# Separate raw tiles for two kinds of expert weights, and one partial result written out by a DMA of its own

## The chip, the cores and the metric

The kernel runs on one core of a Trainium2 chip. The metric is the device time of one execution in microseconds (us). The engines are named as in the profile: PE is TensorE (PEld its weight load), DVE is VectorE, ACT is ScalarE, POOL is GpSimd, SP is SyncE, which here only issues DMAs. Each engine runs its own instructions in order and waits for the others by semaphores.

## What is computed

```python
def reference(**kwargs):
    ...
    attn_out = _attn_ref(**attn_kwargs)            # linear attention, 2 x 8 heads, 576 tokens, 64 wide
    x = np.ascontiguousarray(attn_out.transpose(0, 2, 1, 3)).reshape(B * S, H * D)   # 1152 x 512
    x = _moe_ref(x=x, **moe_kwargs)                # ((x @ w1) * (x @ w2)) @ w3 @ w_out
    return _moe2_ref(x=x, **moe2_kwargs)

def _moe2_ref(x, domain_probs, w1, w2):            # w1: 4 x 512 x 1024, w2: 4 x 1024 x 512
    p = domain_probs / (domain_probs.sum(-1, keepdims=True) + 1e-09)
    out = np.zeros((N, D), dtype=np.float32)
    for e in range(E):
        h = np.maximum(x @ w1[e], 0.0)
        out += p[:, e:e + 1] * (h @ w2[e])
    return out.astype(np.float32)
```

## The kernel before

The program has three stages that overlap at their borders. First the attention runs over eight pairs of heads, and beside it the weights of the gated block are loaded and prepared. Then `gated` forms the gated hidden activations, and `expert_input` multiplies them by the folded product of w3 and w_out; it is called twice, as c0 for batch 0 and c1 for batch 1, and its results are the tiles `x2`. Then come eight expert rounds: four experts, two halves of the hidden width each. Counted from 0, round 0 is `fresh` (it writes the result, the later ones add to it) and round 7 is `last`.

Every matrix is a float32r pair of a high part (made on ACT, line 79) and a low part (made on DVE, line 80, or on POOL); this is `split`, and a product takes three passes (`PASSES`). The matrix products of the expert rounds use a seven-product scheme in place of eight: `hidden` makes the products X1 to X7 and Y1 to Y7 in the order of the list `ORDER`, with sums and differences of blocks formed beforehand in place (line 586, in `raw` for the weights and in `hd` for the activations).

A round does this. `load_w1` loads two raw tiles (512 KB each, by SP, line 611), splits the first (`w1e`), splits a quarter (`w1f`), forms four sums in place, splits the second raw tile, forms more, and splits the first raw tile again: three `w1e` tiles of 8 KB per partition and one `w1f` tile of 4 KB. `hidden(w1t, 0)` and `hidden(w1t, 1)` multiply (line 690) and leave the activations in `hd`. `sums` splits them into `hs` and `hq`. `load_w2` loads two raw tiles and makes four `w2e` tiles. `second` multiplies by them (line 772), once for each half q of the main tokens, and `tails` does the remaining tokens (line 799).

All raw tiles come from one pool, `raw_p`, with three buffers, on the left side of the memory. The other tiles of the expert rounds lie on the right side, where the pools of the gated block (`w1_p`, eight tiles of 4 KB, then `w3_p`, eight tiles of 4 KB, then the temporaries `xq_p` of `expert_input`) are given back; a new tile waits for the old tiles under it (`reuse_waits="tile"`). The `w1e` pool of before takes 4 x 8 + 4 = 36 KB per partition there. The order of the instructions on each engine is set by a scheduler at build time.

In `second` a bank of the accumulator holds 512 columns. The bank of product 1 collects products 1, 6, 7 and 4 in its first half (a chain: each product is added to what the ones before left), and after each of these four steps the intermediate sum is read out, scaled by the routing weight. The row tile `o` (512 columns) of the one batch, `o1`, takes steps 1 and 6 (ACT, line 746) and then the whole bank of product 5 (DVE, line 749). The row tile of the other batch, `o5`, takes the result of product 5 (ACT) and, in its columns `D1`, step 7 of the chain on top (DVE, `add_scaled`, line 749); step 4 goes to its columns `D0` (ACT). A finished row tile is added to the output by a DMA that POOL issues (line 724, `add_to`), which waits for the DMA that wrote the same rows before. There are six `o` buffers, and nine row tiles in a round: four of `second` with q = 0, one of `tails`, four of `second` with q = 1. In round 7 the row tiles are read back from the output first, DVE adds all steps, and SP stores them.

Of the kernel before, what the change touches and what calls it, by code (L numbers as in the profile page):

```python
# [8 lines left out]
F32 = mybir.dt.float32  # L9
# [8 lines left out]
HS_BUFS = 4  # L18
O_BUFS = 6
# [25 lines left out]
def attention_moe_kernel(ctx: ExitStack, tc: tile.TileContext, q, k, v, omega, mw1, mw2, mw3, mwo, probs, ew1, ew2, out):  # L45
# [6 lines left out]
    P = 128  # L52
# [21 lines left out]
    def bank(tag):  # L74
        return ps_p.tile([P, 512], F32, tag=tag, name="ps_" + tag, bufs=BANKS[tag])
# [44 lines left out]
    def out_rows(t):  # L120

        if t == R:
            return [(slice(b * TAIL, (b + 1) * TAIL), slice(b * S + MAIN, (b + 1) * S, 1)) for b in range(B)]
        b, r = (0, t) if t < R else (1, t - R - 1)
        return [(slice(0, P), slice(b * S + r, b * S + MAIN, R))]
# [9 lines left out]
    w12, hid, wo, w3o, x2, xf = {}, {}, [], [], {}, {}  # L135
# [108 lines left out]
    with ExitStack() as actx:  # L244
        at = actx.enter_context(tc.tile_pool(name="at", bufs=2))
        st = actx.enter_context(tc.tile_pool(name="st", bufs=1))
        D1 = D + 1
# [73 lines left out]
        ps = bank("x")  # L321
        transpose(ps[:, :M], om_raw.rearrange("m j d -> m (j d)"))
        for j in range(2):
            s = slice(j * D, (j + 1) * D)
# [27 lines left out]
        class Pair:  # L352
# [81 lines left out]
            def place(self):  # L434
                ps = bank("et")
                for r in range(R):
                    transpose(ps[:, r * P:(r + 1) * P], self.xs[:, r].rearrange("p j d -> p (j d)"))
                x, s = xt[self.b][self.i], MAIN_COLS
                split(x[:, HI, s], x[:, LO, s], ps)
# [100 lines left out]
                    else:  # L540
                        gated(at, 2, int(s[1]), int(s[2]), ("w", "po") * 2)

    raw_p = ctx.enter_context(tc.tile_pool(name="raw", bufs=3, reuse_waits="tile"))
    h_p = mctx.enter_context(tc.tile_pool(name="h", bufs=2 * KF + 2 * KD - XT_BUFS, reuse_waits="tile"))
    a_p = cctx.enter_context(tc.tile_pool(name="a", bufs=1, reuse_waits="tile", side="right"))
    for s in AFTER.split():
# [23 lines left out]
    GH = KE // 4  # L570
    HD = DM // 2
    CH = 2 * P

    def right(name, bufs):
        return ctx.enter_context(tc.tile_pool(name=name, bufs=bufs, side="right", reuse_waits="tile"))

    w1e_p, w2_p, hid_p, hs_p, s_p, o_p = right("w1e", 4), right("w2e", 4), right("hid", 1), right("hs", HS_BUFS), right("s", 2), right("o", O_BUFS)
    hd = hid_p.tile([P, 2 * GH, B, S], F32, name="hd")
    turn = [0]

    def next_bank():
        turn[0] += 1
        return bank(("t", "f", "kv", "et", "f", "x", "w", "po")[turn[0] % 8])
# [4 lines left out]
    def parts(t, src):  # L588
        split(t[:, HI], t[:, LO], src)
        return t  # L590

    def combine(low, high, x11, x12, x21, x22, first, both):


        t = {}
        a = both(low)
        t["A11"], t["A12"] = a[0], a[1]
        t["A22"] = first(x22)
        place(x22, x21, x22, ALU.add)
        place(x21, x11, x21, ALU.subtract)  # L600
        a = both(high)
        t["S3"], t["S1"] = a[0], a[1]
        place(x11, x22, x11, ALU.subtract)
        place(x12, x12, x11, ALU.subtract)
        a = both(low)
        t["S2"], t["S4"] = a[0], a[1]
        return t

    def raw_half(src):
        r = raw_p.tile([P, 2, 512], F32, tag="raw", name="raw")  # L610
        nc.sync.dma_start(out=r.rearrange("p a (k f) -> p (a k) f", f=src.shape[2]), in_=src)
        return r

    def load_w1(hf):

        r = []
        for m in range(2):
            f0 = m * (EFF // 2) + hf * GH * P
            r.append(raw_half(ew1[e, :, f0:f0 + GH * P].rearrange("(k p) f -> p k f", p=P)))

        def both(src):
            t = parts(w1e_p.tile([P, 2, 2, 512], F32R, tag="w1e", name="w1e"), src)
            return [t[:, :, k].rearrange("p a (k f) -> p a k f", k=2) for k in range(2)]

        def first(src):
            t = parts(w1e_p.tile([P, 2, 512], F32R, tag="w1f", name="w1f", bufs=1), src)
            return t.rearrange("p a (k f) -> p a k f", k=2)

        return combine(r[0], r[1], r[0][:, 0], r[0][:, 1], r[1][:, 0], r[1][:, 1], first, both)

    def load_w2(hf):

        r = []
        for m in range(2):
            f0 = m * (EFF // 2) + hf * GH * P
            r.append(raw_half(ew2[e, f0:f0 + GH * P].rearrange("(g p) d -> p g d", p=P)))
        b = {(m, n): r[m][:, :, n * HD:(n + 1) * HD] for m in range(2) for n in range(2)}

        def both(src):
            return parts(w2_p.tile([P, 2, GH, DM], F32R, tag="w2e", name="w2e"), src)  # L640

        t = {}

        def named(x, one, two):
            t[one], t[two] = x[:, :, :, :HD], x[:, :, :, HD:]

        t["both"] = both(r[0]), both(r[1])
        named(t["both"][0], "B11", "B12")
        named(t["both"][1], "B21", "B22")
        place(b[0, 0], b[0, 1], b[0, 0], ALU.subtract)  # L650
        place(b[0, 1], b[1, 1], b[0, 1], ALU.subtract)
        named(both(r[0]), "T1", "T3")
        place(b[1, 1], b[1, 1], b[0, 0], ALU.subtract)
        place(b[1, 0], b[1, 0], b[1, 1], ALU.subtract)
        named(both(r[1]), "T4", "T2")
        return t
# [65 lines left out]
    def add_to(t, d, src, fresh):  # L722
        for n, (rows, toks) in enumerate(out_rows(t)):
            dma = nc.gpsimd.dma_start(out=out[toks, d], in_=src[rows], **({} if fresh else dict(accum_op=ALU.add))).ins  # L724
            if not fresh:
                tc.add_manual_dep(dma, added[t, n].name, after, reason="sum")
            added[t, n] = dma

    def results(t, last):

        o = o_p.tile([P, DM], F32, tag="o", name="o")
        if last:
            for n, (rows, toks) in enumerate(out_rows(t)):
                dma = nc.sync.dma_start(out=o[rows], in_=out[toks]).ins
                tc.add_manual_dep(dma, added[t, n].name, after, reason="sum")
        return o

    def store(t, src):
        for rows, toks in out_rows(t):
            nc.sync.dma_start(out=out[toks], in_=src[rows])  # L740

    def scaled(o, ps, t, last):
        if last:
            add_scaled(o, ps, t)
        else:
            nc.scalar.activation(out=o, in_=ps, func=ACTF.Copy, scale=pr[:, t, e:e + 1])  # L746

    def add_scaled(o, ps, t):
        nc.vector.scalar_tensor_tensor(out=o, in0=ps, scalar=pr[:, t, e:e + 1], in1=o, op0=ALU.mult, op1=ALU.add)  # L749

    D0, D1, DD = slice(0, HD), slice(HD, DM), slice(0, DM)

    def second(w2t, t, q, fresh, last):

        state = {}, {}
        finish = (lambda t, o: store(t, o)) if last else (lambda t, o: add_to(t, DD, o, fresh))
        if last:
            for j in range(2):
                for k, n in (("1", 0), ("5", R + 1)):
                    state[j]["o" + k] = results(n + q * 2 + j, True)  # L760
        for o in ORDER:
            j, k = "XY".index(o[0]), o[1]
            ta, tb = q * 2 + j, R + 1 + q * 2 + j
            now = state[j]
            if k in "15":
                now[k] = next_bank()
            bk = now["1" if k in "1674" else "5"]
            ps = bk[:, D1 if k in "53" else D0]
            a, b = NAMES[k]
            for g in range(GH):  # L770
                for n, (x, y) in enumerate(PASSES):
                    nc.tensor.matmul(  # L772
                        out=ps, lhsT=t[a][:, x, g, j * P:(j + 1) * P], rhs=w2t[b][:, y, g],
                        start=(k in "15" and g == 0 and n == 0), stop=(k in "234" and g == GH - 1 and n == 2),
                        skip_group_check=True,
                    )
            if k in "15" and not last:
                now["o" + k] = results(ta if k == "1" else tb, False)
            if k in "16":
                scaled(now["o1"][:, D0 if k == "1" else D1], ps, ta, last)  # L780
            elif k in "54":
                scaled(now["o5"][:, D1 if k == "5" else D0], ps, tb, last)
                if k == "4":
                    finish(tb, now["o5"])
            elif k == "3":
                add_scaled(now["o1"], bk, ta)
                finish(ta, now["o1"])
            elif k == "7":
                add_scaled(now["o5"][:, D1], ps, tb)

    def tails(w2t, fresh, last):

# [17 lines left out]
    for e in range(NE):  # L810
        for hf in range(2):
            fresh, last = e == 0 and hf == 0, e == NE - 1 and hf == 1
# [42 lines left out]
```

## Time and profile before

| | us |
|---|---|
| three runs | 694.33, 694.74, 696.3 |
| median | 694.74 |
| the profiled execution | 693.17 |
| its span, first to last instruction | 691.4 |
| PE busy | 665.8 |
| DVE busy | 482.7 |
| ACT busy | 402.9 |
| POOL busy | 163.8 |

The profiled execution lies 1.57 us under the median, and 1.8 us of it lie around the span. Busy times are sums over stages with different limits, so a stage is read by itself: which engine is without a gap there, and what the gaps of the others wait for. Times in the text are counted from the start of the span.

### The profile page before, as it was taken

How to read it: one execution, taken by the hardware profiler on the slowest of the kernel's cores; microseconds unless marked ns; L12 is line 12 of the kernel's file. 1: busy time of each engine (PE TensorE's matmuls, PEld its weight loads, DVE VectorE, ACT ScalarE, POOL GpSimd, SP SyncE). 2: the span in 40 equal slices, each digit the busy share in tenths (PEclk: the TensorE clock that was granted, in tenths of full speed). 3: DMA queues.
4: the chain of work that ended last, by engine and by line, in shares of the span. 5: the costliest groups of instructions: out<-in, count | busy, mean ns of one | idle time of the engine just before them, and what ended most of it. 6: DMA issues, size and time to landing. Idle time of an engine off the chain costs nothing.

```text
span 691.4 us, 12448 instructions
## 1 busy us (share of the span) xinstructions
PE 665.8 (96%) x4889; PEld 634.7 (92%) x4889; DVE 482.7 (70%) x782; ACT 402.9 (58%) x867; POOL 163.8 (24%) x155
## 2 busy tenths in 40 slices
PE   7898999999999999998999999999999999999997
PEld 6786778899999999998989999999999999999996
DVE  4888646669593222258987869877888688688795
ACT  5895445565452222246866676677676676686640
POOL 2865223259271000000021122230320311202200
PEclk9999999999999999999999999999999999999999
DMA  9764323235330000001143166372660762745715
GB/s 260 262 210 140 94 91 116 77 113 153 123 92 1 1 1 1 1 1 61 62 137 122 17 122 122 44 150 68 122 137 2 138 123 27 140 93 100 146 32 167
DMA packets 47146, 66.91 MB, mean 97 GB/s; under 512 B 7600, under 2 KB 30128, under 8 KB 47088
## 3 DMA queue, kind: packets, MB, share of 16 engines
q1 hardware_dynamic: 37792, 49.05, 22.8%
q0 software_dynamic: 8608, 16.52, 15.9%
q8 instruction: 38, 0.62, 0.4%
q10 hardware_dynamic: 688, 0.56, 0.3%
q14 instruction: 20, 0.16, 0.1%
HBM read 47.24 MB, written 18.87 MB: 96 GB/s over the span
## 4 chain that ended last, share of the span: by engine, by line
PE 73%; DVE 11%; DMA 6%; ACT 5%; issue 3%; POOL 1%; DVEq 0%; ACTq 0%; POOLq 0%; SPq 0%
PE ps_po L185 5%; PE ps_f L690 5%; PE ps_f L772 4%; DMA raw<-in_moe_w_dram 3%; PE ps_w L158 3%; PE ps_w L690 3%; PE ps_f L158 3%; PE ps_po L158 3%; PE ps_x L690 3%; PE ps_et L690 3%; PE ps_kv L690 2%; PE ps_t L690 2%; PE ps_po L690 2%; PE ps_kv L772 2%; PE ps_kv L412 2%
## 5 line engine op out<-in xcount | busy, mean ns | idle before, releaser
L724 POOL DMA_DIRECT2D out_dram<-o x70 | 57.7, 892 | 382.5 <-DVE o L749 206.6
L93 POOL TENSOR_SCALAR f64e<-f 128x512 f32<-128x512 f32 x40 | 66.8, 1673 | 78.1 <-DVE w3f L95 32.2
L80 DVE TENSOR_TENSOR hs<-hd,hs 128x1024 fp32r<-128x1024 f32 x48 | 58.4, 1219 | 3.1 <-ACT hs L79 2.4
L79 ACT ACTIVATE hs<-hd 128x1024 fp32r<-128x1024 f32 x48 | 50.7, 1056 | 7.9 <-DVE hd L586 4.9
L185 PE MATMUL ps_po<-wo,w3T 128*128 128x512 f32 x192 | 48.4, 400 | 3.3 <-DVE w3T L80 2.8
L690 PE MATMUL ps_f<-x,w1e 128*128 128x288 f32 x288 | 48.2, 298 | 3.1 <-DVE w1e L80 3.1
L674 ACT ACTIVATE hd<-hd 128x288 f32<-128x288 f32 x96 | 41.3, 439 | 15.6 <-DVE hd L672 14.9
L586 DVE TENSOR_TENSOR raw<-raw 128x512 f32<-128x512 f32 x64 | 43.9, 686 | 8.4 <-DMA raw<-in_moe_w_dram 8.1
L185 PEld LDWEIGHTS ps_po<-wo,w3T 128*128 128x128 f32 x192 | 34.8, 188 | 12.2 <-DVE w3T L80 3.9
L690 PEld LDWEIGHTS ps_f<-x,w1e 128*128 128x128 f32 x288 | 41.8, 191 | 3.7 <-DVE w1e L80 3.6
L94 DVE SCALAR_TENSOR_TENSOR f64e<-f,f64e 128x512 uint32<-128x512 uint32 x40 | 40.1, 1012 | 6.1 <-POOL f64e L93 5.8
L586 DVE TENSOR_TENSOR hd<-hd 128x512 f32<-128x512 f32 x64 | 43.9, 685 | 0.6
L79 ACT ACTIVATE w2e<-raw 128x1024 fp32r<-128x1024 f32 x32 | 33.5, 1058 | 17.7 <-PE ps_f L772 4.7
L772 PE MATMUL ps_f<-w2e,hs 128*128 128x256 f32 x288 | 42.6, 283 | 1.0 <-ACT o L746 0.6
L80 DVE TENSOR_TENSOR w2e<-raw,w2e 128x1024 fp32r<-128x1024 f32 x32 | 38.9, 1219 | 4.6 <-ACT w2e L79 4.5
L80 DVE TENSOR_TENSOR w1e<-raw,w1e 128x1024 fp32r<-128x1024 f32 x24 | 29.3, 1222 | 17.5 <-ACT w1e L79 17.2
L772 PEld LDWEIGHTS ps_f<-w2e,hs 128*128 128x128 f32 x288 | 38.1, 191 | 1.5 <-ACT o L746 0.8
L158 PE MATMUL ps_w<-xt,w 128*128 128x288 f32 x144 | 34.4, 298 | 0.0
L79 ACT ACTIVATE w1e<-raw 128x1024 fp32r<-128x1024 f32 x24 | 25.4, 1059 | 15.2 <-DMA raw<-in_moe_w_dram 10.3
L158 PE MATMUL ps_po<-xt,w 128*128 128x288 f32 x144 | 33.9, 296 | 0.0
L79 ACT ACTIVATE hid<-a 128x288 fp32r<-128x288 f32 x32 | 13.0, 440 | 30.8 <-DVE a L169 30.8
L80 POOL TENSOR_TENSOR w<-w12f,w 128x512 fp32r<-128x512 f32 x16 | 22.0, 1384 | 15.1 <-ACT w L79 15.0
(263 smaller groups left out, 1777.4 us busy)
## 6 DMA issues: line engine op xcount, KB each, us to landing
f<-in_moe_w_dram SPq DMA_DIRECT2D x32, 512.0 KB, 3.7
raw<-in_moe_w_dram SPq DMA_DIRECT2D x32, 512.0 KB, 5.5
out_dram<-o POOLq DMA_DIRECT2D x56, 256.0 KB, 5.2
f<-in_moe_w_out_dram SPq DMA_DIRECT2D x8, 512.0 KB, 5.1
kr<-in_k_dram SPq DMA_DIRECT2D x8, 256.0 KB, 3.8
vr<-in_v_dram SPq DMA_DIRECT2D x8, 256.0 KB, 5.0
o<-out_dram SPq DMA_DIRECT2D x8, 256.0 KB, 3.6
out_dram<-o SPq DMA_DIRECT2D x8, 256.0 KB, 2.5
```

The lines of the kernel that those rows point to most:

```text
L79: nc.scalar.activation(out=hi, in_=src, func=ACTF.Copy)
L80: (eng or nc.vector).tensor_tensor(out=lo, in0=src, in1=hi.bitcast(F32), op=ALU.subtract)
L93: nc.gpsimd.tensor_scalar(out=e.bitcast(F32), in0=high.bitcast(F32), scalar1=0.0, scalar2=None, op0=ALU.mult)
L94: nc.vector.scalar_tensor_tensor(out=e, in0=low, scalar=29, in1=e, op0=ALU.logical_shift_right, op1=ALU.bitwise_or)
L158: nc.tensor.matmul(out=bs[c][:, :HS], lhsT=w12[w, g][:, x, kk], rhs=xt[b][kk][:, y, c * HS:(c + 1) * HS], start=(kk == 0 and n == 0), stop ...
L185: nc.tensor.matmul(out=po, lhsT=wt[:, a, g * P:(g + 1) * P], rhs=wo[hf * 4 + g][:, c], start=(n == 0), stop=(n == 3 * KF - 1),)
L412: nc.tensor.matmul(out=ps[:, j * D1:(j + 1) * D1], lhsT=e, rhs=a, start=(r == 0), stop=(r == R))
L586: nc.vector.tensor_tensor(out=o, in0=x, in1=y, op=op)
L674: nc.scalar.activation(out=h, in_=src, func=ACTF.Relu)
L690: nc.tensor.matmul(out=ps, lhsT=w1t[a][:, x, kk, g * P:(g + 1) * P], rhs=x2[b, kk][:, y, s], start=(k in "125" and kk == 0 and n == 0), st ...
L724: dma = nc.gpsimd.dma_start(out=out[toks, d], in_=src[rows], **({} if fresh else dict(accum_op=ALU.add))).ins
L772: nc.tensor.matmul(out=ps, lhsT=t[a][:, x, g, j * P:(j + 1) * P], rhs=w2t[b][:, y, g], start=(k in "15" and g == 0 and n == 0), stop=(k in ...
```

## The change

Raw tiles: `raw_p` is used for the first kind of weights alone and has two buffers in place of three. The second kind gets a pool of its own, `r2`, with two buffers, on the right side behind `w2e`. The `w1e` pool has three tiles in place of four and so takes 28 KB.

Step 7: in rounds 0 to 6 it is no longer added to `o5` by DVE. ACT scales it into a tile of its own, `o7` (128 x 256, four buffers), and after the DMA of `o5` POOL issues a second DMA that adds `o7` to the columns `D1` of the same rows. It waits for the DMA of `o5`. In round 7 step 7 is as before.

```diff
-    raw_p = ctx.enter_context(tc.tile_pool(name="raw", bufs=3, reuse_waits="tile"))
+    raw_p = ctx.enter_context(tc.tile_pool(name="raw", bufs=2, reuse_waits="tile"))
...
-    w1e_p, w2_p, hid_p, hs_p, s_p, o_p = right("w1e", 4), right("w2e", 4), right("hid", 1), right("hs", HS_BUFS), right("s", 2), right("o", O_BUFS)
+    w1e_p, w2_p, r2_p = right("w1e", 3), right("w2e", 4), right("r2", 2)
+    hid_p, hs_p, s_p, o_p = right("hid", 1), right("hs", HS_BUFS), right("s", 2), right("o", O_BUFS)
...
-    def raw_half(src):
-        r = raw_p.tile([P, 2, 512], F32, tag="raw", name="raw")
+    def raw_half(pool, src):
+        r = pool.tile([P, 2, 512], F32, tag="raw", name="raw")
...
-            r.append(raw_half(ew1[e, :, f0:f0 + GH * P].rearrange("(k p) f -> p k f", p=P)))
+            r.append(raw_half(raw_p, ew1[e, :, f0:f0 + GH * P].rearrange("(k p) f -> p k f", p=P)))
...
-            r.append(raw_half(ew2[e, f0:f0 + GH * P].rearrange("(g p) d -> p g d", p=P)))
+            r.append(raw_half(r2_p, ew2[e, f0:f0 + GH * P].rearrange("(g p) d -> p g d", p=P)))
...
                 if k == "4":
                     finish(tb, now["o5"])
+                    if not last:
+                        add_to(tb, D1, now["o7"], False)
...
+            elif k == "7" and last:
+                add_scaled(now["o5"][:, D1], ps, tb)
             elif k == "7":
-                add_scaled(now["o5"][:, D1], ps, tb)
+                now["o7"] = o_p.tile([P, HD], F32, tag="o7", name="o7", bufs=4)
+                scaled(now["o7"], ps, tb, last)
```

The scheduler orders the instructions anew from the first weight split on. On DVE the work on the first round's w1 stands, before the change, in the last splits of c1 (`t` and `x` are its temporaries and results, `p` are kept partial sums of `hidden`):

```order
L226 TENSOR_TENSOR t_3428<-b_3458,t_3428 128x288
L80 TENSOR_TENSOR w1e<-raw,w1e 128x1024
L80 TENSOR_TENSOR w1f<-raw,w1f 128x512
L80 TENSOR_TENSOR x_3291<-b_3458,x_3291 128x288
L80 TENSOR_TENSOR x_3289<-t_3429,x_3289 128x288
L80 TENSOR_TENSOR x_3288<-t_3428,x_3288 128x288
L586 TENSOR_TENSOR raw<-raw 128x512
```

After the change it stands on DVE ahead of and among the splits of c0, some 50 us of matmuls earlier (`a` and `hid` belong to the last call of `gated`, `xf` is c0's result):

```order
L169 TENSOR_TENSOR a<-ps_po,a 128x288
L80 TENSOR_TENSOR w1e<-raw,w1e 128x1024
L80 TENSOR_TENSOR w1f<-raw,w1f 128x512
L80 TENSOR_TENSOR hid<-a,hid 128x288 x2
L587 TENSOR_TENSOR raw<-raw 128x512
L80 TENSOR_TENSOR x_2982<-xf,x_2982 128x288
L587 TENSOR_TENSOR raw<-raw 128x512 x3
L80 TENSOR_TENSOR w1e<-raw,w1e 128x1024
L80 TENSOR_TENSOR x_3012<-xf,x_3012 128x288
L80 TENSOR_TENSOR w1e<-raw,w1e 128x1024
```

All of the first round's w1 work moved there: three wide splits, one half-wide one and four sums. On ACT, in `second` of round 0, the steps of the chains stand like this before (`ht` belongs to `tails`):

```order
L79 ACTIVATE hs<-hd 128x1024
L79 ACTIVATE w1e<-raw 128x1024
L79 ACTIVATE hs<-hd 128x1024
L746 ACTIVATE o<-ps_x,pr 128x256
L746 ACTIVATE o<-ps_w,pr 128x256
L79 ACTIVATE ht<-hd 128x512
```

And with the change, where `o_3861` and `o_3875` are the two `o7` tiles:

```order
L79 ACTIVATE hs<-hd 128x1024
L747 ACTIVATE o_3861<-ps_x,pr 128x256
L79 ACTIVATE w1e<-raw 128x1024
L747 ACTIVATE o_3875<-ps_w,pr 128x256
L79 ACTIVATE hs<-hd 128x1024
L747 ACTIVATE o<-ps_x,pr 128x256
L747 ACTIVATE o<-ps_w,pr 128x256
L79 ACTIVATE ht<-hd 128x512
```

The two new steps came in among the wide splits, one of them with a wide split ahead of it, and the two chains' last steps now stand behind both. On POOL the first call of `second` in round 3 issues its DMAs before the change like this (one number stands for one tile; the last row is that of `tails`):

```order
L724 DMA out_0_dram<-o_5423 128x512
L724 DMA out_0_dram<-o_5441 128x512
L724 DMA out_0_dram<-o_5450 128x512
L724 DMA out_0_dram<-o_5432 128x512
L724 DMA out_0_dram<-o_5556 64x512 x2
```

And with the change:

```order
L725 DMA out_0_dram<-o_5468 128x512
L725 DMA out_0_dram<-o7_5505 128x256
L725 DMA out_0_dram<-o_5477 128x512
L725 DMA out_0_dram<-o_5450 128x512
L725 DMA out_0_dram<-o_5459 128x512
L725 DMA out_0_dram<-o7_5519 128x256
L725 DMA out_0_dram<-o_5587 64x512 x2
```

Three whole-row DMAs stand behind a half-row one there; in the first calls of rounds 1, 2 and 4 one does, and in the other ten calls none.

## Rows read from the trace of the kernel before

**Rows 1.** The page: busy time, share of the span and instructions of each engine.

```profile
PE 665.8 (96%) x4889; PEld 634.7 (92%) x4889; DVE 482.7 (70%) x782; ACT 402.9 (58%) x867; POOL 163.8 (24%) x155
```

**Rows 2.** Stretches: length, busy of PE, PEld, DVE, ACT, POOL; PEclk, DMA share, GB/s.

```profile
260.00:300.00 40.00, 40.00 (x304) 40.00 (x303) 10.52 (x25) 11.37 (x27) 0.00 (x0) 1.00 0.00 1
...
310.00:316.00 6.00, 3.48 (x15) 3.48 (x16) 5.33 (x10) 3.33 (x8) 0.00 (x0) 0.72 0.00 1
...
450.00:500.00 50.00, 49.50 (x379) 48.64 (x378) 39.23 (x56) 35.35 (x69) 10.39 (x12) 1.00 0.53 107
```

**Rows 3.** Timeline of PE at the seam: start, duration, instruction, count, idle before.

```profile
303.34 3.32 PE L204 MATMUL ps_w<-hid,w3o 128*128 128x288 f32 x24
306.50 3.32 PE L204 MATMUL ps_po<-hid,w3o 128*128 128x288 f32 x24
312.52 1.81 PE L690 MATMUL ps_f<-x,w1e 128*128 128x288 f32 x6 [2.71 <-DVE w1e L80]
...
323.34 0.96 PE L690 MATMUL ps_kv<-x,w1e 128*128 128x288 f32 x6
```

**Rows 4.** Timeline of DVE at the same place.

```profile
311.24 1.23 DVE L80 TENSOR_TENSOR w1e<-raw,w1e 128x1024 fp32r<-128x1024 f32 x1
312.39 0.68 DVE L80 TENSOR_TENSOR w1f<-raw,w1f 128x512 fp32r<-128x512 f32 x1
...
313.36 0.82 DVE L80 TENSOR_TENSOR x<-t,x 128x288 fp32r<-128x288 f32 x2
...
317.93 0.45 DVE L672 TENSOR_TENSOR hd<-ps_w,p 128x288 f32<-128x288 f32 x1
318.30 0.68 DVE L586 TENSOR_TENSOR raw<-raw 128x512 f32<-128x512 f32 x1
318.89 1.22 DVE L80 TENSOR_TENSOR w1e<-raw,w1e 128x1024 fp32r<-128x1024 f32 x1
```

**Rows 5.** Waits of PE from 320 us on: total, times, longest.

```profile
PE ps_et L690 <- DVE w1e L80: 1.1, 1, 1.1
...
PE ps_w L772 <- DVE o L749: 0.9, 1, 0.9
...
PE ps_x L772 <- ACT o L746: 0.2, 1, 0.2
```

**Rows 6.** Timeline of PE, three waits inside the expert rounds.

```profile
504.71 0.98 PE L772 MATMUL ps_f<-w2e,hs 128*128 128x256 f32 x6 [0.55 <-ACT o L746]
...
551.02 0.98 PE L772 MATMUL ps_w<-w2e,hs 128*128 128x256 f32 x6 [0.31 <-ACT o L746]
...
597.99 0.98 PE L772 MATMUL ps_et<-w2e,hs 128*128 128x256 f32 x6 [0.97 <-ACT o L746]
```

**Rows 7.** Timeline of ACT ahead of the third of them.

```profile
595.89 1.06 ACT L79 ACTIVATE w1e<-raw 128x1024 fp32r<-128x1024 f32 x1 [1.71 <-DMA raw<-in_moe_w_dram]
...
597.48 0.47 ACT L746 ACTIVATE o<-ps_et,pr 128x256 f32<-128x256 f32 x1
```

**Rows 8.** Groups by line and shape: busy, mean ns; idle before, releasers.

```profile
L746 ACT ACTIVATE o<-ps_f,pr 128x256 f32<-128x256 f32 x29 | 13.7, 472 | 9.8 <-PE ps_f L772 8.3 <-DMA out_dram<-o 1.4
...
L749 DVE SCALAR_TENSOR_TENSOR o<-ps_f,pr,o 128x256 f32<-128x256 f32 x11 | 5.3, 480 | 0.7 <-PE ps_f L772 0.7
```

**Rows 9.** Tile view of out_dram: duration min/median/max of an issue; who waited; landing.

```profile
L724 POOL DMA_DIRECT2D out_dram<-o x70: 539/866/1338, 347.7 to 649.2; - x70
...
  ACT o L746: 3.1, 3
...
DMA to landing us min/median/max: 2.0/4.4/9.0
```

**Rows 10.** Timeline of POOL, one call's row sums in the fourth round.

```profile
485.13 0.86 POOL L724 DMA_DIRECT2D out_dram<-o  x1 [18.62 <-DVE raw L586]
491.05 2.63 POOL L724 DMA_DIRECT2D out_dram<-o  x3 [5.07 <-ACT o L746]
```

**Rows 11.** Tile view of raw, from issue of a weight load to landing.

```profile
DMA to landing us min/median/max: 3.3/5.2/8.5
```

## The prediction

> **What bounds the kernel now.** I read the page first: PE is busy 665.8 us [rows 1] of the span's 691.4, so the whole kernel has some 26 us in which PE does nothing, and only that can be won, unless a stage is rebuilt. Next come the stretches: from 260 to 300 us PE is busy without a gap while DVE and ACT work a quarter of the time, and from 310 to 316 us PE is busy 3.48 of 6 us at a granted clock of 0.72 [rows 2]. So the seam between c1 and the first expert round is the place with the largest hole, and the two engines that could have filled it were idle just ahead of it. The timeline of PE shows the hole itself [rows 3], that of DVE what PE waited for [rows 4]. For the rest of the expert rounds I read what PE waits for from 320 us on: 13 rows, from 1.1 us down to 0.2 us, 7.1 us in all, of which the 1.1 and one of 0.4 are still the seam; of the other 5.6 us ScalarE's row steps (o) have 2.8, ScalarE's relu (hd) 1.1, DVE's o 0.9 in the last round, DVE's splits 0.8 (the first, the last and one between are in [rows 5]). The reader should see that PE never waited for DVE's step 7 outside the last round: the step that is moved is not one that PE is late for.
>
> **The seam, the largest term.** One 24-matmul group of c1 takes 306.50 - 303.34 = 3.16 us, so six matmuls of this shape take 0.79 us. The last group of c1 would be followed at 306.50 + 3.16 = 309.66 us; the first expert matmul starts at 312.52, after 2.71 us of waiting for the split of w1e, and its six take twice their time or more. Nine groups of six lie between 309.66 and 323.34 us [rows 3]: 13.68 us for 9 x 0.79 = 7.11 us of work, so 6.57 us are lost (waiting for w1's splits three times, and the half clock of 1.2 GHz after the first wait).
>
> Why so late? In the code the w1e pool takes 36 KB and lies over the eight tiles of w1_p (32 KB) and one tile of w3_p, which c1 still multiplies by; with 28 KB it lies over w1_p alone, which is free when the last `gated` is done. In the changed order all this work (three wide splits, a half-wide one, four sums) stands in c0, where DVE and ACT have some 29 of 40 us free [rows 2]; it takes on DVE 3 x 1.15 + 0.6 + 4 x 0.6 = 6.4 us by the distances of the starts in [rows 4]. So I cost it at nothing there. If that cover were gone, c0's copies out of the banks would come late, and PE would lose at most those 6.4 us.
>
> What is late next? The T products need c1's last splits. They start at 313.36 with 1.8 us of w1 splits ahead of them [rows 4]; without these they end near 312.4, and the changed order of PE needs them after five groups, at 309.66 + 5 x 0.79 = 313.6. Then w2: its raw tiles now lie where w3_p and the temporaries of c1 were, so their loads can't start before 309.7 to 312.5 (before, one was loaded early). A weight load lands after 5.2 us, at most 8.5 [rows 11], so at some 317.5 us. In the changed order ten additions (0.37 apart), seven sums (0.6), seven wide splits (1.15) and one half-wide one stand on DVE up to the second activation split that `second` needs [rows 4]: 3.7 + 4.2 + 8.05 + 0.6 = 16.6 us. Two of them are done by 314.5, the third waits for product X3 until 309.66 + 10 x 0.79 = 317.6, so the others end at 317.6 + 15.8 = 333.4 if the load is in time. PE has 26 groups ahead of `second` (330.2) and reaches the product in question about 3.2 us later, at 333.4. There is no slack there, so I let 0 to 2.7 us of the 6.57 come back (the upper end is the size of the first hole) and take 1.2. **Seam: -5.4 us.**
>
> **Own raw tiles in the rounds.** Three PE waits of 0.55, 0.31 and 0.97 us [rows 6] are ScalarE's fault only at second hand: ahead of the last, ScalarE stood 1.71 us waiting for a raw load, then split, and read out the bank 1.6 us later [rows 7]; ahead of the other two the same pair of a raw load and a wide split stands on its timeline. With its own two tiles a w1 load can be issued as soon as the round before has made its last w1e split, most of a round ahead, and no longer behind w2's tiles. On SP's queue the loads stand in pairs, w1 and w2 in turn, so none blocks the other kind for long. I take all three away: **-1.8 us** (bounds 0, as far as other work is late behind them, and 2.2, by the starts of PE's groups). The third w1e tile that is missing is wanted for the next round's first split, which waits for the last use of A11 and A12 in `hidden(w1t, 1)`; the order puts that split among the activation splits, behind that use, as before.
>
> **Step 7.** 28 instructions (4 in each of 7 rounds) leave DVE, 480 ns each, 13.4 us; ACT gets 28 of 472 ns, 13.2 us [rows 8], in rounds in which it is 71% busy and DVE 78% [rows 2]. Nothing of that is on the path by itself, as PE waits for an accumulator bank only if four groups do not cover the read. Bounds: a gain of 0.8 us (the PE waits for DVE's splits), and a loss of all 13.2 us. The nearest row is what ACT's 119 row steps cost PE now: 2.8 us, less the 1.8 above, so 1.0 us, 8 ns each; 28 more of them, and ACT's other waits a little longer, make **+0.5 us**.
>
> **The new DMAs.** POOL issues 28 more, 0.87 us each (at most 1.34) [rows 9], on an engine that does nothing else from 320 us on: 24 us beside the 58 of the 70 that it issues there now, in some 330 us. Each waits for the DMA of `o5` to land, 4.4 us, at most 9.0 [rows 9], and POOL's queue stands meanwhile. Behind it are the DMAs of `tails`, whose tile is wanted six tiles later, and in rounds 1 to 4 one or three whole rows. The worst is round 3; there the first row sum went out at 485.13 us and the other three from 491.05 on [rows 10], so the wait of about 5 us falls into a gap of 5 us that is there anyway. ACT waits for such tiles in three places already, 3.1 us in all [rows 9]. Bounds 0 and 4 us, taken **+0.4 us**, near the row of the gap.
>
> On issuing, the Trainium skill speaks against the change: "SBUF — State Buffer", section "SBUF: two separate sides" and the one behind it, says that POOL can't write the descriptors of its DMAs while DVE holds the port that they share, and gives about 3.1 us in place of 0.62 for one such DMA beside a copy. The trace disagrees for the DVE work here: with DVE 78% busy [rows 2] no issue took over 1.34 us [rows 9]. By the page's figure, as an estimate, 98 issues of 3.1 us would fill the whole of the expert rounds.
>
> **Sum.** 693.17 (the profiled execution) - 5.4 - 1.8 + 0.5 + 0.4 = 686.9 us; the median of the runs lies 1.57 us above the profiled execution, so **688.4 us**. A measurement can tell 0.3%, 2.1 us, from no change: faster means under 692.7, slower over 696.8.
>
> **Rivals.** *The wait moves to w2.* What stood at w1e now stands at w2e, because its loads can't start before c1 is done. If they start at 313 and take the longest landing, 8.5 us [rows 11], they come at 321.5 in place of 317.5, and DVE, which has no slack there, hands 4 us more to PE: 692.4. Against it speaks that most of these tiles lie over w3_p, free at 309.7, and that SP has nothing else to do. 0.14.
>
> *ScalarE gives it back.* The order is new in all rounds; if the remaining waits of PE (5.6 - 1.8 = 3.8 us) double because ACT's queue is fuller and step 4 of both chains now stands behind two more reads and a wide split, the time is 692.2. For it: PE's waits name ACT more than any other. Against: DVE, the fuller engine, loses the same 13 us. 0.12.
>
> *POOL's queue holds the row tiles (slower).* Place: the first five row steps of the second call of `second`, which follow each other on ACT and need tiles that the first call's DMAs free. Price: a half-row DMA waits 4.4 to 9.0 us [rows 9] with whole rows behind it. In three places there is no cover already [rows 9]; if each tile comes 9.0 later in three rounds, or 4.4 in six, ACT stands some 27 us, and PE with it: 715 at worst. It decides when more than 8.4 us of these reach PE (688.4 to 696.8). The order speaks against it: only in round 3 do rows that the second call takes stand behind a half row, and there the gap covers it. 0.08.
>
> "DMA: Bandwidth & Descriptors", section "Anatomy of one DMA", in the Trainium skill gives 2.0 us + bytes/436e3 for such a DMA, an estimated 2.6 us for 256 KB; by that this rival could not reach 27 us but some 8 to 16. The trace has 4.4 [rows 9], and I keep its price.
>
> *All closes.* The seam loses nothing and half of the 3.8 us go too, as DVE gets 13 us and its waits for ACT's late w1 splits go: 693.17 - 6.57 - 1.8 - 1.9 + 1.57 = 684.5. 0.11.
>
> *It doesn't do what it says*: the early split can't be, as its tile comes free too late. But it stands ahead of c0's reads in ACT's queue, and a tile free only after c1 would block c1 itself. Under 0.01.
>
> **How the numbers follow.** The forecast has 0.55: 686.0 to 691.0. Faster: 0.55 + 0.11 + about half of each of the two middle rivals, 0.13, makes 0.79; the other half of these is within 0.3%, 0.13; slower 0.08. The range leaves out the slow rival and a little at each end: 684.0 to 692.8.
>
> **What would show it.** Right: PE without a wait over 0.3 us between 306 and 320 us, at a granted clock of 1.00; w1e splits at about 259 us on DVE; no wait of ACT for raw loads in the rounds; `second` starting near 331 in place of 337. Wrong in the second term: ACT still waiting for raw loads. Wrong in step 7 or the DMAs: PE's waits for ACT's row steps above 3 us in all, or ACT waiting for out_dram's DMAs for well over 3.1 us. The forecast is wrong as a whole if PE stands as long at w2e's splits as it stood at w1e's.

## The result

| | before | after |
|---|---|---|
| runs beside each other, us | 694.33 to 696.3 (4) | 683.14 to 685.67 (4) |
| median, us | 694.8 | 684.63 |
| the profiled execution, us | 693.17 | 684.2 |
| its span, us | 691.4 | 682.4 |

The changed kernel is faster: the ratio of the times is 0.9848 (95% interval 0.9824 to 0.9873). In a later comparison, six runs beside eleven of the kernel before, it was 0.9854 (0.9813 to 0.9894; medians 686.05 and 695.02 us). The forecast was 688.4 us with a range of 684.0 to 692.8: the time lies inside, 3.8 us under the forecast.

The page of after, the row that answers to [rows 1]; the step moved 28 instructions from DVE (782 to 754) to ACT (867 to 895), and POOL issues 28 DMAs more:

```profile
PE 661.4 (97%) x4889; PEld 632.6 (93%) x4889; DVE 470.5 (69%) x754; ACT 413.9 (61%) x895; POOL 187.9 (28%) x183
```

The stretches of after (columns as in [rows 2]). From 260 to 300 us DVE and ACT now have 32 and 31 instructions in place of 25 and 27, PE is still without a gap, and from 310 to 316 us PE is busy all 6 us at a granted clock of 1.00, where it was 3.48 at 0.72:

```profile
260.00:300.00 40.00, 40.00 (x304) 40.00 (x303) 16.73 (x32) 14.86 (x31) 0.00 (x0) 1.00 0.09 27
310.00:316.00 6.00, 6.00 (x47) 6.00 (x47) 4.24 (x12) 4.18 (x11) 0.00 (x0) 1.00 0.14 24
450.00:500.00 50.00, 50.00 (x390) 49.52 (x389) 37.16 (x53) 36.08 (x71) 13.00 (x15) 1.00 0.60 108
```

The timeline of PE at the seam, which answers to [rows 3]. The last group of c1 starts at 308.51, the first expert group 3.16 us later, with no wait, and each group of six keeps its 0.8 us. The first product of `second` starts at 331.57, and some 3 us on stands a new wait for DVE's split of the activations:

```profile
308.51 3.32 PE L204 MATMUL ps_po<-hid,w3o 128*128 128x288 f32 x24
311.67 0.96 PE L691 MATMUL ps_f<-x,w1e 128*128 128x288 f32 x6
312.48 0.96 PE L691 MATMUL ps_kv<-x,w1e 128*128 128x288 f32 x6
...
331.57 0.87 PE L773 MATMUL ps_x<-w2e,hs 128*128 128x256 f32 x6
...
335.50 0.95 PE L773 MATMUL ps_po<-w2e,hs 128*128 128x256 f32 x6 [0.76 <-DVE hs L80]
```

The splits that PE waited for in [rows 4] at 311 us are done on DVE 50 us earlier, in c0 (timeline of DVE, after):

```profile
262.13 1.23 DVE L80 TENSOR_TENSOR w1e<-raw,w1e 128x1024 fp32r<-128x1024 f32 x1 [0.39 <-ACT w1e L79]
263.27 0.69 DVE L80 TENSOR_TENSOR w1f<-raw,w1f 128x512 fp32r<-128x512 f32 x1
263.88 0.82 DVE L80 TENSOR_TENSOR hid<-a,hid 128x288 fp32r<-128x288 f32 x2
```

What PE still waits for from 300 us on (the view of [rows 5]; us in total, times, longest) is six rows of 3.2 us in all, where from 320 us on alone it was 7.1 us in 13 rows:

```profile
PE ps_kv L691 <- ACT o L747: 1.3, 1, 1.3
PE ps_po L773 <- DVE hs L80: 0.8, 1, 0.8
PE ps_w L773 <- DVE o L750: 0.3, 1, 0.3
PE ps_t L773 <- ACT hd L675: 0.3, 1, 0.3
PE ps_po L773 <- ACT o L747: 0.3, 1, 0.3
PE ps_t L773 <- ACT o L747: 0.2, 1, 0.2
```

**An account of PE's lost time** makes kernels comparable that start their expert rounds at different moments. From c1's last group on, the distance of the starts of successive groups on PE's timeline, less the pure pace of its matmuls (0.1317 us for 288 columns, from the 3.16 us of 24 in [rows 3]; 0.12 and 0.233 us for 256 and 512 columns, from groups that follow each other without a wait), is what PE lost there. Before it lost 17.15 us, after 6.14: 11.0 us less. The profiled times differ by 9.0 us only, since in after's execution c1's last group started 2.0 us later (308.51 for 306.50). So the whole gain lies behind c1, and 2 us of it were hidden by the front of the program in that one execution (the last section shows that this is chance). All kernels do the same matmuls behind c1, so an error of the pace would shift every sum by the same amount and leave the differences.

### The profile page after: what moved, and what is told of

Read it like the earlier page. It is cut to its first block, busy times and chain, and to the rows that moved or that the text cites. A ratio compares the mean times of both kernels' runs of the same rounds, so it can differ in the third digit from the quotient of the medians.

```text
span 682.4 us, 12480 instructions
## 1 busy us (share of the span) xinstructions
PE 661.4 (97%) x4889; PEld 632.6 (93%) x4889; DVE 470.5 (69%) x754; ACT 413.9 (61%) x895; POOL 187.9 (28%) x183
## 4 chain that ended last, share of the span: by engine, by line
PE 82%; DVE 7%; DMA 4%; ACT 2%; issue 2%; SPq 1%; POOL 1%; DVEq 0%; ACTq 0%; POOLq 0%
PE ps_f L691 6%; PE ps_f L773 6%; PE ps_po L185 5%; PE ps_x L691 3%; PE ps_w L691 3%; PE ps_et L691 3%; PE ps_w L158 3%; PE ps_f L158 3%; PE ps_kv L691 3%; PE ps_po L158 3%; PE ps_t L691 3%; PE ps_po L691 3%; PE ps_x L773 3%; PE ps_et L773 3%; PE ps_t L773 3%; PE ps_kv L773 3%
## 5 line engine op out<-in xcount | busy, mean ns | idle before, releaser
L725 POOL DMA_DIRECT2D out_dram<-o x98 | 81.9, 904 | 354.8 <-DVE o L750 172.5
L691 PE MATMUL ps_f<-x,w1e 128*128 128x288 f32 x288 | 46.2, 294 | 0.0
```

Of the source, the lines that this page charges most:

```text
L691: nc.tensor.matmul(out=ps, lhsT=w1t[a][:, x, kk, g * P:(g + 1) * P], rhs=x2[b, kk][:, y, s], start=(k in "125" and kk == 0 and n == 0), st ...
```

## The experiments

The account for all kernels, in us, by stretches of time: "seam" is the first 16.9 us from the start of c1's last group (c1's end and the first products of round 0), "round 0" the next 35.4, "round 7" the last 44.5. The first column says where the first stretch of a kernel starts.

| kernel | c1's last group | seam | round 0 | rounds 1 to 6 | round 7 | sum |
|---|---|---|---|---|---|---|
| before | 306.50 | 6.59 | 2.98 | 5.86 | 1.72 | 17.15 |
| after | 308.51 | 0.15 | 2.53 | 2.31 | 1.15 | 6.14 |
| after_again | 312.09 | 0.14 | 2.53 | 2.33 | 1.24 | 6.24 |
| w1e3_only | 308.88 | 0.81 | 2.93 | 3.82 | 1.33 | 8.89 |
| w1e3_pad | 311.91 | 6.20 | 3.04 | 3.87 | 1.37 | 14.48 |
| raw_only | 307.26 | 0.14 | 3.34 | 3.81 | 1.64 | 8.93 |
| w1e3_step7 | 309.28 | 0.82 | 2.17 | 2.33 | 1.42 | 6.74 |
| o7_dve | 313.31 | 0.14 | 3.29 | 3.39 | 0.33 | 7.15 |
| no_o7_dma | 310.44 | 0.15 | 2.53 | 2.33 | 1.47 | 6.48 |
| act_twice | 310.69 | 0.14 | 2.55 | 5.68 | 1.02 | 9.39 |
| o7b2 | 308.39 | 0.14 | 2.53 | 2.33 | 0.10 | 5.10 |
| o7b2_again | 310.91 | 0.14 | 2.53 | 2.33 | 0.12 | 5.12 |
| s7_o8 | 307.72 | 0.80 | 2.17 | 2.33 | 0.25 | 5.55 |

The two executions of the changed kernel agree within 0.02 us in each of the first three stretches, though c1 ended 3.6 us apart; round 7, which reads from memory, differs by 0.09.

### The smaller pool of w1e alone

```diff
-    ... = right("w1e", 4), right("w2e", 4), ...
+    ... = right("w1e", 3), right("w2e", 4), ...
```

> The kernel before with three w1e tiles in place of four and nothing else: the three raw tiles stay shared and step 7 stays on DVE. Theory A (the pool of 28 KB lies over w1_p alone, so the first round's w1 is ready before c1 ends): the seam closes, PE loses under 1 us between c1 and the first product of second in place of 6.5, and ScalarE's waits for raw loads in the rounds stay near 10 us; 687 to 689 us. Rival C (the shared raw tiles held the seam up: w2's load takes the third tile): the seam stays at 6 to 6.5 us, 693 to 696 us.

Measured: 687.35 us, ratio 0.9857 (0.9814 to 0.99). The seam is closed; the timeline of PE in this kernel:

```profile
308.88 3.32 PE L204 MATMUL ps_po<-hid,w3o 128*128 128x288 f32 x24
312.04 0.96 PE L690 MATMUL ps_f<-x,w1e 128*128 128x288 f32 x6
```

One number, 3 in place of 4, brings 8.26 of the 11.0 us: 5.8 in the seam, 2.0 in rounds 1 to 6, 0.4 in the last. And with three shared raw tiles, as before, ACT's waits for raw loads are gone too, where the expectation let them stay near 10 us. Before, this row stood among ACT's waits from 320 us on, and in w1e3_only there is none:

```profile
ACT w1e L79 <- DMA raw<-in_moe_w_dram: 10.3, 6, 2.2
```

ACT's timelines show why. In the kernel before, the first w1 split for the next round stood 25.8 us ahead of the split of `w1f` that follows it, and waited for its load:

```profile
502.61 1.06 ACT L79 ACTIVATE w1e<-raw 128x1024 fp32r<-128x1024 f32 x1 [2.06 <-DMA raw<-in_moe_w_dram]
...
528.36 0.62 ACT L79 ACTIVATE w1f<-raw 128x512 fp32r<-128x512 f32 x1
```

With three w1e tiles no fourth one is free so early, and the split stands 7.4 us ahead of that of `w1f`, without a wait for its load:

```profile
516.65 1.06 ACT L79 ACTIVATE w1e<-raw 128x1024 fp32r<-128x1024 f32 x1
...
524.07 0.64 ACT L79 ACTIVATE w1f<-raw 128x512 fp32r<-128x512 f32 x1
```

### The same pool, moved over w3_p again

An unused tile of 8 KB ahead of the pool, so that three w1e tiles lie again over a tile that c1 still multiplies by:

```diff
+    pad_p = right("pad", 1)
+    pad = pad_p.tile([P, 2048], F32, name="pad")
+    nc.gpsimd.memset(pad[:, :8], 0.0)
     ... = right("w1e", 3), right("w2e", 4), ...
```

> As the run with three w1e tiles alone, but with an unused tile of 8 KB ahead of the w1e pool, so that the pool lies from 8 to 36 KB and again over one tile of w3_p. Theory A: the seam opens again, 6 to 6.5 us lost, 693 to 696 us, as before. A rival that puts the gain down to fewer tiles or to another order in general: the seam stays closed, 687 to 689 us.

Measured: 693.78 us, ratio 0.9959 (0.9931 to 0.9988). The hole of [rows 3] is back with the same 2.71 us, and the groups behind it start 0.90 and 1.41 us apart in place of 0.80:

```profile
311.91 3.32 PE L204 MATMUL ps_po<-hid,w3o 128*128 128x288 f32 x24
317.94 1.08 PE L693 MATMUL ps_f<-x,w1e 128*128 128x288 f32 x6 [2.71 <-DVE w1e L80]
318.84 1.62 PE L693 MATMUL ps_kv<-x,w1e 128*128 128x288 f32 x6
320.25 1.65 PE L693 MATMUL ps_x<-x,w1e 128*128 128x288 f32 x6
```

It loses 6.20 us in the seam and, in rounds 1 to 6, 3.87, as without the pad (3.82). So the seam is a matter of where the tiles lie, and the gain in the rounds is not: that one comes with their number.

### Own raw tiles without step 7

The changed kernel with step 7 added to `o5` by DVE as before (`o7` and its DMA taken out).

> The changed kernel with step 7 undone (DVE adds it into the row tile, no DMA of its own); three w1e tiles and own raw tiles stay. Theory A (step 7 costs a little or nothing, the raw tiles bring the rest): seam closed, no wait of ScalarE for raw loads, 683 to 685.5 us, as fast as the changed kernel or faster. Rival B (what was won in the rounds beyond the three raw waits comes from the 13 us that DVE lost): PE loses 3 to 5 us more in the rounds than in the changed kernel, 687.5 to 689.5 us.

Measured: 687.09 us, ratio 0.9848 (0.9799 to 0.9897); it loses 8.93 us, beside 8.89 with shared raw tiles. Own raw tiles bring 0.67 us in the seam and lose 0.41 in round 0 and 0.31 in round 7: nothing, in sum. The time lies between the two expectations: the changed kernel loses 2.79 us less, a little under the 3 to 5 of the rival. No kernel here has own raw tiles beside four w1e tiles, so whether they alone would have taken ACT's waits for raw loads away is open.

### Step 7 without own raw tiles

The kernel before with three w1e tiles and the change of step 7.

> The kernel before with three w1e tiles and with step 7 on ScalarE with its own DMA; the three raw tiles stay shared. Theory A: the raw waits of ScalarE stay, step 7 costs up to 1 us: 687.5 to 690 us, as the run with three w1e tiles alone or slower. Rival B: DVE's 13 us bring 3 us in the rounds without own raw tiles too: 684 to 686 us.

Measured: 684.01 us, ratio 0.9798 (0.9746 to 0.985). Against w1e3_only it loses 6.74 in place of 8.89 us, so step 7 on ACT brings 2.15 us; with own raw tiles (raw_only to after) 2.79. Ahead of round 7, in which step 7 is as before, the two differences are 2.24 and 2.30. The forecast had it cost 0.9 with its DMAs. The waits of PE from 320 us on show what goes; in w1e3_only, where all of them are 0.2 to 1.1 us:

```profile
PE ps_t L772 <- ACT hd L674: 1.1, 1, 1.1
PE ps_x L690 <- DVE w1e L80: 0.7, 1, 0.7
PE ps_t L690 <- DVE w1e L80: 0.7, 1, 0.7
```

and in w1e3_step7, where no w1e split is left among them, and one wait for ACT has come in:

```profile
PE ps_kv L690 <- ACT o L746: 1.3, 1, 1.3
PE ps_t L772 <- ACT hd L674: 1.1, 1, 1.1
PE ps_w L772 <- DVE o L749: 0.6, 1, 0.6
```

### Is it DVE's relief, or the shorter chain?

Moving step 7 did two things: 28 reads left DVE, and the step no longer follows product 5 in one row tile. Here DVE writes `o7`:

```diff
-                scaled(now["o7"], ps, tb, last)
+                nc.vector.tensor_scalar(out=now["o7"], in0=ps, scalar1=pr[:, tb, e:e + 1], scalar2=None, op0=ALU.mult)
```

> The changed kernel, but the new tile of step 7 (o7) is written by DVE in place of ACT; its DMA stays. Theory 1 (moving step 7 helped because 28 reads of 0.48 us left DVE, which PE waits for at w1's splits): the reads are back on DVE, PE loses 8.5 to 9.5 us from c1's last group on in place of 6.1, waits of PE for DVE's w1e splits of about 0.7 us come back, and the time is about 687. Theory 2 (it helped because step 7 no longer has to follow product 5 in the same row tile): PE loses 6 to 7 us, no wait for w1e splits, time about 684.6.

Measured: 685.74 us, ratio 0.984 (0.98 to 0.9881); PE loses 7.15 us, between the two. Round 7, in which step 7 is as it was, accounts for much of that: 0.33 in place of 1.64. In the stretches ahead of it the kernel loses 0.14 + 3.29 + 3.39 = 6.82 us, where raw_only loses 7.29 and after 4.99. So of 2.30 us the shorter chain has 0.47, and moving the reads from DVE to ACT 1.83. The second part holds the new order too: at 604 of the 2808 places in PE's order from c1's last group on, after and o7_dve multiply other tiles, and relief and order were not separated. The waits for w1's splits came back, as the first theory had it:

```profile
PE ps_kv L691 <- DVE w1e L80: 0.7, 1, 0.7
PE ps_x L691 <- DVE w1e L80: 0.4, 1, 0.4
```

### More of the same on ACT

```diff
                 scaled(now["o7"], ps, tb, last)
+                scaled(now["o7"], ps, tb, last)
```

> The changed kernel with the read into o7 done twice on ACT, the second over the first: 28 more instructions of 0.47 us, 13 us more on ACT, DVE as it is. If ACT has room in the rounds (8 ns of PE's time for a read, as the prediction costed step 7): 0.2 us slower, PE loses 6 to 7 us, time 684.6 to 685.5. If ACT is the engine next in line (it is about 74% busy there): the waits of PE for ACT's reads at least double, PE loses 8 us or more, time 686.5 or more.

Measured: 688.53 us, ratio 0.9876 (0.9836 to 0.9917). Rounds 1 to 6 lose 5.68 us in place of 2.31. The 28 added reads cost PE some 3.3 us, 0.12 us each and not 8 ns, in an order of PE's products that differs from that of after at 721 of the 2808 places. The busy times of a stretch inside the rounds fit a kernel in which ACT had no room for more. The stretch of w1e3_only, of after and of act_twice, in this order (PE, PEld, DVE, ACT, POOL as in [rows 2]):

```profile
360.00:640.00 280.00, 277.72 (x2137) 273.36 (x2136) 223.94 (x322) 195.04 (x377) 51.61 (x61) 1.00 0.49 97
```

```profile
360.00:640.00 280.00, 278.51 (x2148) 274.77 (x2147) 214.98 (x300) 206.40 (x405) 73.07 (x87) 1.00 0.59 107
```

```profile
360.00:640.00 280.00, 277.63 (x2122) 272.02 (x2122) 211.21 (x295) 211.69 (x424) 71.12 (x84) 1.00 0.59 106
```

With DVE busy 224 and ACT 195 of 280 us, PE loses 3.82 us in rounds 1 to 6; with 215 and 206 it loses 2.31; with 211 and 212 it loses 5.68. As the order is made anew for each kernel, the price of one read is not a constant, and that the balance of the two engines decides is argued from three points, not shown.

### Without the new DMAs

```diff
                     finish(tb, now["o5"])
-                    if not last:
-                        add_to(tb, D1, now["o7"], False)
```

> The changed kernel without the 28 DMAs that add o7 to the output: step 7 of the chain is computed and read out, and is missing in the result in rounds 0 to 6. If the new DMAs cost nothing on the path: PE loses 6.1 us as in the changed kernel, its 1.3 us wait for ACT near 580 us stays (ACT is held there by a split that waits for PE), time 684 to 685. If POOL's queue holds row tiles, as the prediction's +0.4 us and its slow rival have it: ACT's 3.0 us of waits for out_dram's DMAs shrink to nothing and PE gains 0.4 to 1.6 us, time 683 to 684.2.

Measured: 685.49 us, ratio 0.9834 (0.9795 to 0.9872). The account is that of the changed kernel to 0.02 us up to round 7 (0.15, 2.53, 2.33), and the 1.3-us wait near 580 us stays. The 28 DMAs cost PE nothing there. They do hold POOL: in the changed kernel's tile view of out_dram (as in [rows 9]) POOL waited 62.5 us for DMAs to land, and ACT 3.0 us for row tiles:

```profile
L725 POOL DMA_DIRECT2D out_dram<-o x98: 542/857/1438, 343.6 to 647.9; - x98
...
  POOL out_dram L725: 62.5, 24
...
  ACT o L747: 3.0, 2
...
DMA to landing us min/median/max: 2.0/4.6/8.3
```

They hold row tiles too. Most of ACT's 3.0 us, and 4.43 us of DVE, are one place in round 2, a wait for the DMA that frees a tile (timelines of DVE and ACT, after):

```profile
450.97 0.75 DVE L750 SCALAR_TENSOR_TENSOR o<-ps_w,pr,o 128x512 f32<-128x512 f32 x1 [4.43 <-DMA out_dram<-o]
```

```profile
451.75 0.47 ACT L747 ACTIVATE o<-ps_f,pr 128x256 f32<-128x256 f32 x1 [2.52 <-DMA out_dram<-o]
```

Without the 28 DMAs both are gone. The one row left of those that wait for out_dram is DVE's, for the loads of round 7:

```profile
  DVE o L750: 3.7, 2
```

So the second expectation was right that ACT's waits vanish, and wrong that PE gains by it: PE has no wait at 451 us with them, and loses the same without them.

### A seventh row tile

```diff
-O_BUFS = 6
+O_BUFS = 7
...
-                now["o7"] = o_p.tile([P, HD], F32, tag="o7", name="o7", bufs=4)
+                now["o7"] = o_p.tile([P, HD], F32, tag="o7", name="o7", bufs=2)
```

> The changed kernel with seven o tiles in place of six and two o7 tiles in place of four, in the same memory; the order of the rounds is the same but for a few rows of the last. If ACT's 3.0 us of waits for out_dram's DMAs reach PE: PE loses up to 1 us less, time 683.6 to 684.3. If they lie in ACT's idle time: the same within 0.5 us, PE's 1.3 us wait near 580 us stays, time 684 to 685.

Measured: 682.41 us, ratio 0.9791 (0.9755 to 0.9827); PE loses 5.10 us. The time lies below both expectations, and neither names the place: rounds 0 to 6 are as in the changed kernel, and the 1.04 us come from round 7. There the row tiles are read back from the output first, by ten loads. With six tiles SP issued seven of them early, one at 665.39 and the last two at 669.03, behind stores (SP's timeline, after):

```profile
627.60 20.65 SPq L735 DMA_DIRECT2D o<-out_dram  x7
...
669.03 1.04 SPq L735 DMA_DIRECT2D o<-out_dram  x2
```

and DVE, and PE behind it, waited for one of them (DVE's and PE's timelines, after):

```profile
672.43 0.48 DVE L750 SCALAR_TENSOR_TENSOR o<-ps_w,pr,o 128x256 f32<-128x256 f32 x1 [2.34 <-DMA o<-out_dram]
```

```profile
672.97 0.98 PE L773 MATMUL ps_w<-w2e,hs 128*128 128x256 f32 x6 [0.31 <-DVE o L750]
```

With seven tiles, eight loads go early, one again at 665.39, and one is left, and PE has no wait in round 7 (SP's timeline of o7b2):

```profile
626.24 24.36 SPq L735 DMA_DIRECT2D o<-out_dram  x8
...
669.26 0.34 SPq L735 DMA_DIRECT2D o<-out_dram  x1
```

The order of a few rows of round 7 changed along with the tile; the two were not separated.

### Beside each other on one chip

The changed kernel, the same with the seventh row tile, and the kernel before with three w1e tiles, step 7 on ACT and eight row tiles, five rounds each.

> The changed kernel once more, on one chip with the two kernels below. Every theory: PE loses 6.1 us from c1's last group on, time 684 to 686, ratio to the kernel before about 0.985.

> The changed kernel with seven o tiles and two o7 tiles. If the seventh row tile is what made it faster (PE's waits for DVE's o in the last round gone): PE loses 5.1 us again, 1 us under the changed kernel beside it, 683 to 685. If the 2 us between the two came from the first 300 us, which differ from run to run: PE loses the same as the changed kernel, times within 0.5 us.

> The kernel before with three w1e tiles, the change of step 7 and eight o tiles; the raw tiles stay three shared ones. If own raw tiles bring nothing: as seven o tiles, within 0.5 us of it, PE loses 5 to 6 us, no wait of ACT for raw loads. If own raw tiles are worth what the prediction gave them: 1.8 us slower than seven o tiles, with waits of ACT for raw loads in the rounds.

Measured: 686.05 us (ratio 0.9854, 0.9813 to 0.9894), 684.13 (0.9844, 0.9806 to 0.9883) and 684.0 (0.9832, 0.9797 to 0.9867). The accounts repeat, 6.24 and 5.12 us, and s7_o8 loses 5.55, with no wait of ACT for raw loads. So own raw tiles are worth some 0.4 us where step 7 is on ACT: 0.66 in the seam, of which round 0 gives 0.36 back, and the rest in round 7. The medians of the two variants lie 2 us under that of the changed kernel, of which the account explains 1.1 and 0.7; the intervals overlap, and a lead over the changed kernel is shown by the account, not by the times.

## Why the forecast was right, and where it was not

**What bounds the kernel: right.** The seam was the largest hole, and the waits inside the rounds the rest.

**The seam: right in cause, mis-sized by 0.7 us.** The pool's place over w3_p was the cause; w1e3_pad shows it by bringing all of it back. Of the 6.57 us, 6.44 are won in the seam itself. The work moved into c0 costs nothing there, as the term had it: from the 450th matmul of the program to c1's last group PE takes 223.13 to 223.21 us in all thirteen traces. The term had 1.2 us come back at the first products of `second`, where it saw no slack. It was the right place and the right time: DVE's split of `hs` was to end at 333.4 us, and ends at 335.35 with c1 2.0 us later, and PE waits 0.76 us for it (335.50). But round 0 behind the seam loses 2.53 us in all where it lost 2.98: of two waits of before there, 0.60 for ACT's `hd` and 0.38 for DVE's `ht`, 0.27 is left. With step 7 still on DVE it loses 3.34 (raw_only), so in sum some 0.4 us came back there, a third of the 1.2, and seam and round 0 together won 6.09 us in raw_only (9.57 less 3.48), for the 5.4 of the term. Moving step 7 won the rest of what round 0 gained.

**Own raw tiles: right in size by luck, wrong in cause.** The three waits of [rows 6] are gone, and rounds 1 to 6 lose 2.0 us less in w1e3_only, beside the 1.8 of the term. But the missing w1e tile is enough for that, and own raw tiles beside it add nothing: raw_only and w1e3_only agree in rounds 1 to 6 (3.81 and 3.82). The step that failed is the sentence that the order puts the next round's first split behind the last use of A11 and A12 "as before". Before, it did not stand there; the fourth tile let the scheduler pull it forward to 502.61, into a wait for its load, as [rows 7] already showed for 595.89. Beside shared raw tiles, a w1e tile more was the harm.

**Step 7: wrong in sign.** The term was a cost of 0.5 us between a gain of 0.8 and a loss of 13.2. It is a gain of 2.15 (w1e3_step7) to 2.79 us (after), beyond the bound on that side. That bound was DVE's split waits in the trace of before. But the missing tile puts w1's splits late in the round, where PE waits for DVE's twice 0.7 us in w1e3_only and no more in w1e3_step7; the relief was worth more in the new order than the old one could show. How much of the gain is the relief, and how much the order that came with it, stays open. The price of a read was no constant either: 8 ns was an average over the reads of before, and in act_twice 28 more cost 0.12 us each.

**The new DMAs: 0.4 taken, nothing measured.** In round 3, the place that the term feared, it went as predicted: behind the first row's landing POOL issues the half row and the two rows that follow it, and no tile is late (POOL's timeline of after, which answers to [rows 10]):

```profile
479.90 0.84 POOL L725 DMA_DIRECT2D out_dram<-o  x1 [13.63 <-ACT o L747]
484.32 2.65 POOL L725 DMA_DIRECT2D out_dram<-o  x3 [3.58 <-DMA out_dram<-o]
```

The place where tiles were late is round 2, at 451 us, and PE didn't wait there. POOL's issues took 0.86 us at the median and 1.44 at most in after, with DVE busy 37 of 50 us. The Trainium skill's figure of 3.1 us ("SBUF — State Buffer", section "A bandwidth-pool intuition that's wrong (but worth ruling out)") is for a DVE `tensor_copy`. From 343 to 648 us DVE runs TENSOR_TENSOR and SCALAR_TENSOR_TENSOR alone, before and after, so no row here tests that figure, and the prediction's "disagrees" goes too far. Its estimate from it, 98 x 3.1 = 304 us, would also not have filled the expert rounds, some 375 us.

**The sum.** The terms were -5.4 - 1.8 + 0.5 + 0.4 = -6.3 us. The account has -11.0: 6.4 in the seam, 0.4 in the rest of round 0, 3.6 in rounds 1 to 6, 0.6 in round 7. The profile gives back 2.0 of them in the front, and the median of after lies 0.43 us over its profiled execution, not 1.57: that makes the 3.8 us to the forecast. By raw_only the first two terms, 7.2 us, won 8.22, and the last two, a cost of 0.9, are a gain of 2.79. Both errors go the same way, so that the time lies inside the range is partly luck: the account's 11.0 us from the median of before would be an estimated 683.7 us, just outside.

**The rivals.** *All closes* had 684.5 and 0.11, and its parts came out: the seam lost nothing, the raw waits went, and DVE's waits for late w1 splits with them. It was given too little, because the sum charged step 7 to ACT and took nothing for DVE's relief. That its time is met to 0.1 us is luck again: its gains add up to 10.3 us, the account's to 11.0. *The wait moves to w2*: PE waits for no w2e split. *POOL's queue* holds row tiles, above all in round 2, and costs PE nothing. *ScalarE gives it back*: one place, the 1.3 us near 580, where a w2e split that waits for PE stands ahead of ACT's row steps (timelines of ACT and PE, after).

```profile
579.31 1.06 ACT L79 ACTIVATE w2e<-raw 128x1024 fp32r<-128x1024 f32 x1 [0.98 <-PE ps_kv L805]
```

```profile
581.94 1.06 PE L691 MATMUL ps_kv<-x,w1e 128*128 128x288 f32 x6 [1.30 <-ACT o L747]
```

**What was to be seen.** No wait of PE over 0.3 us between 306 and 320 at a clock of 1.00: so. Early splits on DVE near 259: at 262.13. No waits of ACT for raw loads: so, for another reason. `second` near 331: 331.57, with c1 2 us later.

## What to carry over

Count the buffers of a pool as a constraint on the order, not as free help: a buffer more can make a scheduler pull a step in front of a load that hasn't landed, and push the pool over memory that is still in use. Price a move of work between two engines in the new order and on both sides: what the relieved engine is late for may only appear once another part of the change has moved its work. And compare kernels by the time that the bounding engine loses behind a common point, when the stretch ahead of it varies more than the effect.

## What was not expected of the hardware

The stretch ahead of the change, whose code is the same in all kernels, is not the same length twice. The first 80 us (columns as in [rows 2]) in the profiled executions of before, of after_again and of o7_dve:

```profile
0.00:80.00 80.00, 69.58 (x431) 58.62 (x433) 57.06 (x99) 55.40 (x152) 42.95 (x43) 1.00 0.67 202
```

```profile
0.00:80.00 80.00, 66.95 (x393) 56.22 (x393) 54.06 (x94) 52.10 (x144) 41.00 (x42) 0.96 0.66 195
```

```profile
0.00:80.00 80.00, 68.67 (x390) 57.54 (x391) 53.68 (x93) 51.07 (x141) 40.96 (x42) 0.94 0.67 195
```

PE issued 431, 393 and 390 matmuls in them, at a mean granted clock of 1.00, 0.96 and 0.94 of 2.4 GHz, and c1's last group started at 306.50, 312.09 and 313.31 us. So up to 6.8 us of a time, more than the size of most terms here, are decided before the first changed instruction, and all of it in the first 90 us: from the 450th matmul, which starts at 83.3 us in before and at 90.2 in o7_dve, to c1's last group the thirteen traces agree within 0.08 us. Before's profiled execution has the earliest start of c1 of them all. PE waits in those 80 us for work in gaps (it is busy 84 to 87% of them), and the clock falls in some executions and not in others; why the gaps differ was not followed.
